# Linear attention and a Strassen MLP in float32 on one core: a longer software pipeline in attention, earlier fetches of weight pieces, later loads of values

## The chip, the core and the metric

The kernel runs on one core of one Trainium2 chip. The metric is the device time of one execution in microseconds (us). It stood at 1071.13 us before the change, the median of three runs (1074.04, 1069.88 and 1071.13). The engines are named as the profile names them: PE is TensorE's matrix multiply and PEld its weight load, DVE is VectorE, ACT is ScalarE, POOL is GpSimd, and SP is the engine whose queue issues nearly all DMAs.

## The reference

Eight batches of eight heads, 576 rows, 64 columns. Attention by 128 random features, then a rank-32 mixing over the rows, then an MLP:

```python
def phi(x):
    proj = np.einsum('bhsd,md->bhsm', x, omega)
    h = proj - np.sum(x * x, axis=-1, keepdims=True) / 2.0
    h = h - np.max(h, axis=-1, keepdims=True)
    return np.exp(h) / np.sqrt(m)
kv = np.einsum('bhsm,bhsd->bhmd', k_p, v)
z = np.sum(k_p, axis=2)
num = np.einsum('bhsm,bhmd->bhsd', q_p, kv)
den = np.einsum('bhsm,bhm->bhs', q_p, z)[..., None] + 1e-06
x = num / den                                  # then [batch, row, head * 64 + column]
u = x + (x.transpose(0, 2, 1) @ U @ V).transpose(0, 2, 1)
out = u + np.maximum(u @ w_ch1, 0.0) @ w_ch2
```

q, k, v and omega are float32. U, V, w_ch1 (512 x 2048) and w_ch2 (2048 x 512) are float64 and are brought to float32 on the chip.

## The kernel before, in words

The program has two stages. Up to about 315 us of the profile it is attention, with the mixing of finished batches and the first part of the weight decoding woven in. From about 345 us to the end it is the MLP, as seven-product (Strassen) block multiplications. The change touches attention alone.

**Units, rounds and steps.** A unit is a pair of batches and a pair of heads; there are 16. Its 2 x 576 rows make nine tiles of 128 rows, one of which (tile 4) holds rows of both batches. Round r works on one unit's keys and one unit's queries side by side, tile by tile, so that there are 16 x 9 = 144 steps (`Step`, lines 728 to 770). Round 0 has two units' keys, the last round two units' queries. One step goes through this chain:

- `turn`, `high`, `low` (lines 610 to 622), once for three tiles: DVE transposes the raw rows into `xT`, ACT rounds them to `xh`, POOL makes the remainder `xl`.
- `project` (lines 734 to 743): six PE matmuls into one PSUM bank `p_p` (two banks, taken in turn), three for keys and three for queries.
- `peak` (line 749): DVE takes the negated maxima `nm` from the bank.
- `exp` (line 756): four ACT activations from the bank into the SBUF tile `e` (a ring of two), the queries' half first.
- `use`: for keys (line 653) two PE matmuls add `e` times the values `vt` (or `vm` in tile 4) to `p_kv`; for queries (line 679) PE transposes `e` into `p_q`.
- `copy` (line 684): DVE or ACT, by the step's parity, copies `p_q` into the SBUF tile `eT` (a ring of four).
- `combine` (lines 692 and 699): PE multiplies `eT` by the finished key sums `kv` into `p_n`.
- `finish` (lines 709 to 726): DVE takes reciprocals (`rec`) and normalizes into `x`.

**What sets the order.** The loop over s (line 826) runs through the steps with a table `DELAY`: at position s the operation `op` is written for step s - DELAY[op]. The order in which a position's operations are written is fixed: turns, copies, exponentials of the queries, norms, exponentials of the keys, mixing, use of the queries, project, use of the keys, peak, combine. A scheduler then makes each engine's instruction list: it takes the written order as priority but lets an instruction that it reckons ready pass one that it reckons waiting. Each engine works its list in order and stops at the first instruction that has to wait.

**Loads.** All loads of a round stand in SP's list. At positions t = 0 and 1 of round r come 16 DMAs of the next keys (`kt`) and queries (`qt`) (line 594). At t = 4 and 5 come the next keys' values (`load_values`, lines 632 to 643, six DMAs `vt` and `vm`). The tiles of values are two, and a third at the start in a spare tile `x`, so a load has to wait until the keys two units earlier are through with their tile.

**Weight decoding.** `decoding` (line 125) is a generator that is advanced once in some steps (two of three at first, later one of two). A piece of float64 words is fetched by SP into one of two tiles `raw` (line 195; 512 KB for a piece of w1), ACT makes its magnitude and its low word (`magnitude`, lines 132 and 135), and DVE follows in three instructions, one for each advance (lines 150, 151, 154). The third is the last reader of `raw`. For the first 11 pieces (`wide`) two empty advances follow, and at the fifth the next fetch into the tile is written:

```python
if j == len(slots) - 1:
    fetch(i + 1 + depth())
```

**Mixing.** When a pair of batches is through, `mixing` (line 390) adds the rank-32 product in 512-column matmuls (lines 446, 411 and 414), DVE adds x into the tile `ut` (line 422, a ring of two), and SP stores it to DRAM.

Of the kernel before, what the change touches and what calls it, by code (L numbers as in the profile page):

```python
# [29 lines left out]
def performer_mlp_kernel(ctx: ExitStack, tc, q, k, v, omega, U, V, w1, w2, out):  # L30
# [85 lines left out]
    def decoding(jobs, late, lean, base, hold=(), defer=(), wide=0):  # L116
# [25 lines left out]
        for i, job in enumerate(jobs):  # L142
# [21 lines left out]
            for j, slot in enumerate(slots):  # L164
# [6 lines left out]
                if j == len(slots) - 1:  # L171
                    fetch(i + 1 + depth())
# [217 lines left out]
    def mixing(pair, x, last):  # L390
# [272 lines left out]
    class Queries(Part):  # L663
# [18 lines left out]
        def copy(self, s):  # L682
            self.eT[s] = wk.tile([P, 2, P], F32, name="eT", bufs=4)
            (nc.vector.tensor_copy if (s + self.place) % 2 else nc.scalar.copy)(out=self.eT[s], in_=self.pq.pop(s))  # L684
# [43 lines left out]
    class Step:  # L728
# [17 lines left out]
        def peak(self):  # L746
# [5 lines left out]
            self.e = wk.tile([P, 4, P], F32, name="e", bufs=2)  # L752
# [56 lines left out]
    for j in range(2):  # L809
# [8 lines left out]
        "turn0": 0, "copy": 5, "turn1": 0, "exp1": 4, "norm": 7, "exp0": 4,  # L818
        "kvfin": 5, "high0": 0, "low0": 1, "high1": 1, "low1": 1, "use1": 4,
        "project": 2, "use0": 4, "peak": 3, "combine": 6,  # L820
    }
    steps = {}
# [3 lines left out]
    for s in range(NR * NT + 7):  # L826
# [3 lines left out]
        if r + 1 < NR:  # L830
# [11 lines left out]
            if t in (4, 5) and not last:  # L842
                new[0].load_values(t - 4)
# [11 lines left out]
        at = lambda op: steps.get(s - DELAY[op])  # L855
        for p in at("turn0").group(0) if at("turn0") else []:
            p.turn()
        if s % (3 if s < 6 * NT else 2):
            advance(decoder)
        st = at("copy")  # L860
        for p in st.queries() if st else []:
            p.copy(st.s)
        for p in at("turn1").group(1) if at("turn1") else []:
            p.turn()
        if at("exp1") and at("exp1").n > 1:
            at("exp1").exp(1)
        st = at("norm")
        for p in st.queries() if st else []:
            if st.s == 0 and p.hp == 0:
                x = xp.tile([P, NT, DM], F32, name="x")  # L870
            p.finish(st.s, x)
            if st.s == 1 - p.last and p.hp == NU - 1:
                mixers.append(mixing(p.pair, x, p.last))
        if at("exp0"):
            at("exp0").exp(0)
        st = at("kvfin")
        for p in st.parts if st and st.s == NT - 1 else []:
            if isinstance(p, Keys):
                p.finish()
        for p in at("high0").group(0) if at("high0") else []:  # L880
            p.high()
        for p in at("low0").group(0) if at("low0") else []:
            p.low()
# [519 lines left out]
```

## Time and profile before

| what | value |
|---|---|
| time, three runs | 1074.04, 1069.88, 1071.13 us; median 1071.13 |
| the profiled execution's own time | 1071.45 us |
| span of the profiled execution, first to last instruction | 1069.5 us |
| outside the span | 1071.45 - 1069.5 = 1.95 us |
| PE busy over the span | 1036.0 us (97%) |
| DVE, ACT, POOL busy | 867.7 us (81%), 614.5 us (57%), 504.1 us (47%) |
| mean granted PE clock | 0.992 |

How to read it: matmuls overlap in the array, so PE's busy time is the union of durations that each hold a pipeline's latency; a PE that is 97% busy can still be short of matmuls. PEld, the time in which weights are being loaded, falls sooner when the list stalls. A wait is shown in brackets at the row of the instruction that waited, with what ended it. The granted clock is 1.00 or 0.50 at any one time; a stage's value is its mean.

### The profile page before, as it was taken

The numbers are of one execution on the slowest core, as the hardware profiler recorded it, in microseconds if no ns is written. First come the engines' busy times: TensorE is split into PE (matmuls) and PEld (weight loads), VectorE is DVE, ScalarE is ACT, GpSimd is POOL, SyncE is SP. The second block draws the span as 40 slices with busy tenths as digits, with TensorE's granted clock in tenths as the row PEclk, the third lists the DMA queues.
The fourth block names the chain that finished last, engine by engine and source line by source line (L and its number), as shares of the span: only waits on it lengthen the run. The fifth ranks groups of instructions, "written<-read, shape, count | busy, mean of one in ns | idle before, by whom it ended". The sixth has DMA issues, their size and how long they took to land. (4 is left out here: it accounts for less than half of the span.)

```text
span 1069.5 us, 23886 instructions
## 1 busy us (share of the span) xinstructions
PE 1036.0 (97%) x8497; PEld 1013.1 (95%) x8497; DVE 867.7 (81%) x1510; ACT 614.5 (57%) x1479; POOL 504.1 (47%) x453
## 2 busy tenths in 40 slices
PE   8899999999998889999999999999999999999998
PEld 7888899989987789999999999999999999999998
DVE  4787898897898976676677476779999999999995
ACT  5887889988874546445355354655344444444442
POOL 3445866866433623233233324535745545545543
PEclk9998999999999999999999999999999999999999
DMA  9688578585335765887677856964455355454451
GB/s 132 137 148 162 107 179 165 119 196 111 85 90 133 194 178 128 225 226 180 192 203 180 226 160 205 313 212 160 167 177 168 131 176 169 138 172 165 139 172 46
DMA packets 380486, 175.51 MB, mean 164 GB/s; under 512 B 275664, under 2 KB 353488, under 8 KB 375760
## 3 DMA queue, kind: packets, MB, share of 16 engines
q1 hardware_dynamic: 378000, 173.70, 61.9%
q8 instruction: 67, 1.10, 0.4%
q10 hardware_dynamic: 2368, 0.30, 0.2%
q14 instruction: 51, 0.42, 0.1%
HBM read 109.97 MB, written 63.96 MB: 163 GB/s over the span
## 5 line engine op out<-in xcount | busy, mean ns | idle before, releaser
L756 ACT ACTIVATE e<-p_p,nm 128x128 f32<-128x128 f32 x576 | 166.9, 396 | 29.6 <-DVE nm L749 22.9
L1176 ACT CAST gh<-gs 128x512 fp32r<-128x512 f32 x140 | 86.7, 621 | 153.7 <-DVE gs L1150 83.1
L1150 POOL TENSOR_TENSOR gs<-graw 128x512 f32<-128x512 f32 x70 | 104.8, 1504 | 145.1 <-DMA graw<-g 88.5
L943 ACT ACTIVATE g<-g 128x512 f32<-128x512 f32 x105 | 66.4, 632 | 165.2 <-DVE g L947 106.3
L622 POOL TENSOR_TENSOR xl<-xT,xh 128x384 fp32r<-128x384 f32 x96 | 97.0, 1027 | 113.0 <-ACT xh L618 101.6
L1183 DVE TENSOR_TENSOR gl<-gs,gh 128x512 fp32r<-128x512 f32 x140 | 134.8, 971 | 15.4 <-ACT gh L1176 13.6
L749 DVE TENSOR_REDUCE nm<-p_p 128x4 f32<-128x512 f32 x144 | 98.1, 681 | 28.7 <-PE p_p L743 17.7
L174 POOL TENSOR_TENSOR wf<-wf,low 128x512 int32<-128x512 int32 (+2 forms) x35 | 45.1, 1289 | 141.3 <-ACT g L943 120.6
L741 PE MATMUL p_p<-omh,xh 128*128 128x256 f32 x288 | 93.8, 326 | 3.2 <-ACT e L756 1.7
L1262 POOL TENSOR_TENSOR u<-u,p 128x256 f32<-128x256 f32 x72 | 74.8, 1068 | 33.3 <-DVE u L1262 30.7
L1176 ACT CAST gh<-graw 128x512 fp32r<-128x512 f32 x107 | 63.9, 619 | 36.9 <-PE p_q L1337 8.9
L1183 DVE TENSOR_TENSOR gl<-graw,gh 128x512 fp32r<-128x512 f32 x107 | 81.1, 773 | 4.9 <-ACT gh L1176 4.0
L743 PE MATMUL p_p<-omh,xl 128*128 128x256 f32 x288 | 82.7, 288 | 0.6 <-POOL xl L622 0.6
L742 PE MATMUL p_p<-oml,xh 128*128 128x256 f32 x288 | 82.3, 286 | 0.0
L1337 PE MATMUL p_p<-wh,gh 128*128 128x256 f32 x288 | 81.1, 282 | 0.0
L1337 PE MATMUL p_p<-wh,gl 128*128 128x256 f32 x288 | 81.0, 281 | 0.0
L1337 PE MATMUL p_p<-wl,gh 128*128 128x256 f32 x288 | 80.9, 281 | 0.0
L699 PE MATMUL p_n<-kv,eT 128*128 128x65 f32 x512 | 73.2, 273 | 6.8 <-ACT eT L684 2.9
L699 PEld LDWEIGHTS p_n<-kv,eT 128*128 128x128 f32 x512 | 68.1, 195 | 10.6 <-ACT eT L684 3.3
L1337 PE MATMUL p_q<-wh,gh 128*128 128x256 f32 x276 | 77.7, 282 | 0.0
L1337 PE MATMUL p_q<-wh,gl 128*128 128x256 f32 x276 | 77.7, 281 | 0.0
L1337 PE MATMUL p_q<-wl,gh 128*128 128x256 f32 x276 | 77.5, 281 | 0.0
(267 smaller groups left out, 4019.3 us busy)
## 6 DMA issues: line engine op xcount, KB each, us to landing
graw<-g SPq DMA_DIRECT2D x36, 1024.0 KB, 5.3
g<-g SPq DMA_DIRECT2D x282, 128.0 KB, 2.4
raw<-in_moe_w_ch_dram SPq DMA_DIRECT2D x22, 512.0 KB, 4.8
u_dram<-ut SPq DMA_DIRECT2D x36, 256.0 KB, 2.4
u<-u_dram SPq DMA_DIRECT2D x36, 256.0 KB, 2.7
out_dram<-u SPq DMA_DIRECT2D x36, 256.0 KB, 2.4
kt<-in_k_dram SPq DMA_DIRECT2D x120, 72.0 KB, 2.7
qt<-in_q_dram SPq DMA_DIRECT2D x120, 72.0 KB, 2.6
```

Of the source, the lines that this page charges most:

```text
L622: nc.gpsimd.tensor_tensor(out=self.xl[-1], in0=self.turned, in1=f32(self.xh[-1]), op=ALU.subtract)
L699: nc.tensor.matmul(pn[:, h, :], eT[:, h, :], kv[:, h, s // 5, :], start=True, stop=True)
L741: nc.tensor.matmul(o, part.xh[g][:, ts], oh, start=True, stop=False)
L742: nc.tensor.matmul(o, part.xh[g][:, ts], ol, start=False, stop=False)
L743: nc.tensor.matmul(o, part.xl[g][:, ts], oh, start=False, stop=True)
L749: nc.vector.tensor_reduce(out=self.nm[:, :n], in_=self.pp[:, :n], axis=AX.X, op=ALU.max, negate=True)
L756: nc.scalar.activation(out=self.e[:, j, :], in_=self.pp[:, j, :], func=AF.Exp, bias=self.nm[:, j : j + 1])
L1150: K(engine.tensor_tensor(out=to, in0=self.val[x], in1=self.val[y], op=op))
L1176: K(nc.scalar.copy(out=h, in_=v))
L1183: K(nc.vector.tensor_tensor(out=l, in0=v, in1=f32(h), op=ALU.subtract))
L1262: K(engine.tensor_tensor(out=out, in0=x, in1=y, op=ALU.add))
L1337: K(nc.tensor.matmul(acc[bank][:, half, :], x[:, ks], y[:, f, :], start=(now.s == 0 and k == 0 and half == 0 and x is h and y is wh), stop ...
```

## The change

Six edits, all in attention:

1. `DELAY` grows: use 4 to 5, copy 5 to 6, `kvfin` (ACT's copy of the finished key sums) 5 to 6, combine 6 to 8, norm 7 to 9. Turns, project (2), peak (3) and exp (4) stay.
2. Over the last 18 steps the delays fall by one for every three steps until they are what they were (`SHORT`), so that the loop still ends at the same position. A position can hold an operation of two steps there.
3. The rings grow with it: `e` from two to three, `eT` from four to six. `p_p` stays at two banks, `p_q` at two.
4. `load_values` moves from t = 4 and 5 to t = 7 and 8 (`VT` is the delay of the keys' use plus two; it was that delay itself).
5. The fetch of a raw piece, for the first 11 pieces, is written behind the third advance of the piece that leaves the tile, and not behind its fifth.
6. The ring of `ut` grows from two to three.

```diff
-                if j == len(slots) - 1:
+                if j == (2 if i < wide else len(slots) - 1):
                     fetch(i + 1 + depth())
...
-                ut = mp.tile([P, DM], F32, name="ut", tag=tag, bufs=2)
+                ut = mp.tile([P, DM], F32, name="ut", tag=tag, bufs=3 if tag == "ut" else 2)
...
-            self.eT[s] = wk.tile([P, 2, P], F32, name="eT", bufs=4)
+            self.eT[s] = wk.tile([P, 2, P], F32, name="eT", bufs=6)
...
-            self.e = wk.tile([P, 4, P], F32, name="e", bufs=2)
+            self.e = wk.tile([P, 4, P], F32, name="e", bufs=3)
...
-        "project": 2, "use0": 4, "peak": 3, "combine": 6,
+        "project": 2, "use0": 5, "peak": 3, "combine": 8,
     }
+    SHORT = {"copy": 5, "norm": 7, "kvfin": 5, "use1": 4, "use0": 4, "combine": 6}
+    CLOSE = NR * NT - 18
+
+    def delay(op, k):
+        return max(SHORT.get(op, DELAY[op]), DELAY[op] - max(0, (k - CLOSE + 3) // 3))
+
+    VT = DELAY["use0"] + 2
...
-            if t in (4, 5) and not last:
-                new[0].load_values(t - 4)
+            if t in (VT, VT + 1) and not last:
+                new[0].load_values(t - VT)
...
-        at = lambda op: steps.get(s - DELAY[op])
...
+        def at(op):
+            for k in range(s - DELAY[op], s - SHORT.get(op, DELAY[op]) + 1):
+                if k in steps and k + delay(op, k) == s:
+                    yield steps[k]
```

The rest of the diff turns each `if at(op)` of the loop into `for st in at(op)`.

What the scheduler makes of it is seen in the engines' lists. First SP's list in the third and fourth round, before the change. `kt` and `qt` are the 16 loads of a round, `vt` and `vm` its values, `raw` a piece of w1:

```order
L594 DMA kt<-in_k_dram 32x18x32 x8
L594 DMA qt<-in_q_dram 32x18x32 x8
L636 DMA vt_120<-in_v_dram 128x4x64 x2
L640 DMA vm_121<-in_v_dram 64x2x64
L636 DMA vt_120<-in_v_dram 128x4x64 x2
L640 DMA vm_121<-in_v_dram 64x2x64
L195 DMA raw<-in_moe_w_ch_dram 128x1024
L594 DMA kt<-in_k_dram 32x18x32 x8
L594 DMA qt<-in_q_dram 32x18x32 x8
L636 DMA vt_122<-in_v_dram 128x4x64 x2
L640 DMA vm_123<-in_v_dram 64x2x64
L195 DMA raw<-in_moe_w_ch_dram 128x1024
```

The same place of SP's list after the change:

```order
L594 DMA kt<-in_k_dram 32x18x32 x8
L594 DMA qt<-in_q_dram 32x18x32 x8
L195 DMA raw<-in_moe_w_ch_dram 128x1024
L636 DMA vt_120<-in_v_dram 128x4x64 x2
L640 DMA vm_121<-in_v_dram 64x2x64
L636 DMA vt_120<-in_v_dram 128x4x64 x2
L640 DMA vm_121<-in_v_dram 64x2x64
L594 DMA kt<-in_k_dram 32x18x32 x8
L594 DMA qt<-in_q_dram 32x18x32 x8
L195 DMA raw<-in_moe_w_ch_dram 128x1024
L636 DMA vt_122<-in_v_dram 128x4x64 x2
```

The first piece of w1 has passed six loads of values and the second has passed three; the loads of keys and queries stand where they stood.

Then PE's list around step 104, before. Here `e_4050` and `eT_4114` belong to step 104, `e_4089` to step 105, and `p_p_4078` to the projection of step 106:

```order
L743 MATMUL p_p_4078<-omh_115,xl_4000 128x256
L653 MATMUL p_kv_3912<-vt0_120,e_4050 128x65 [waits DMAHW3_49]
L653 MATMUL p_kv_3912<-vt0_120,e_4050 128x65 [waits DMAHW4_49]
L699 MATMUL p_n_4174<-kv_3544,eT_4114 128x65 [waits DVE_49,Activation_49]
L699 MATMUL p_n_4174<-kv_3544,eT_4114 128x65
L679 MATMUL p_q_4130<-ident_100,e_4089 128x128 [waits Activation_49] x2
L741 MATMUL p_p_4133<-omh_115,xh_3970 128x256 [waits Activation_49]
```

And after, where `e_4034` and `eT_4132` are step 104's, `e_4073` step 105's, `e_4128` step 106's, and `p_p_4117` is the projection of step 107:

```order
L679 MATMUL p_q_4138<-ident_100,e_4073 128x128 [waits PE_49,Activation_49]
L679 MATMUL p_q_4138<-ident_100,e_4073 128x128 [waits Activation_49]
L741 MATMUL p_p_4117<-omh_115,xh_3947 128x256 [waits DVE_49,Activation_49]
L742 MATMUL p_p_4117<-oml_116,xh_3947 128x256
L743 MATMUL p_p_4117<-omh_115,xl_3977 128x256
L741 MATMUL p_p_4117<-omh_115,xh_3979 128x256
L742 MATMUL p_p_4117<-oml_116,xh_3979 128x256
L743 MATMUL p_p_4117<-omh_115,xl_3981 128x256
L653 MATMUL p_kv_3916<-vt0_120,e_4034 128x65 [waits DMAHW3_49]
L653 MATMUL p_kv_3916<-vt0_120,e_4034 128x65 [waits DMAHW4_49]
L699 MATMUL p_n_4221<-kv_3554,eT_4132 128x65 [waits DVE_49,PE_49]
L699 MATMUL p_n_4221<-kv_3554,eT_4132 128x65
```

The use of step 104's keys and its combine have moved behind the projection of step 107; the transposes of step 105 stand, as before, between the projections of steps 106 and 107. Counted over steps 10 to 125 (116 steps), the newest projection ahead of a step's transposes is the next step's in all 116 cases in both lists. Ahead of the use of a step's keys it is that of two steps on in all 116 cases before, and of three (114) or four (2) after. Ahead of a combine it is that of two steps on 86 times and of three 30 times before, 76 times and 40 times after. ACT's and DVE's copies stand by the same exponentials and maxima as before, bar single cases. Behind attention PE's list is the same, row by row, apart from buffer numbers.

More of the change, by code (lines that the diff above doesn't have):

```diff
@@ L854, in performer_mlp_kernel @@
             early.todo.append(None)
[L855 to L857 removed]
+        def at(op):
+            for k in range(s - DELAY[op], s - SHORT.get(op, DELAY[op]) + 1):
+                if k in steps and k + delay(op, k) == s:
+                    yield steps[k]
+        for st in at("turn0"):
+            for p in st.group(0):
+                p.turn()
         if s % (3 if s < 6 * NT else 2):
@@ L859, in performer_mlp_kernel @@
             advance(decoder)
[L860 to L883, printed above, removed]
-        for p in at("high1").group(1) if at("high1") else []:
-            p.high()
+        for st in at("copy"):
+            for p in st.queries():
+                p.copy(st.s)
@@ new lines, in performer_mlp_kernel @@
+        for st in at("turn1"):
+            for p in st.group(1):
+                p.turn()
+        for st in at("exp1"):
+            if st.n > 1:
+                st.exp(1)
+        for st in at("norm"):
+            for p in st.queries():
+                if st.s == 0 and p.hp == 0:
+                    x = xp.tile([P, NT, DM], F32, name="x")
+                p.finish(st.s, x)
+                if st.s == 1 - p.last and p.hp == NU - 1:
+                    mixers.append(mixing(p.pair, x, p.last))
@@ L886, in performer_mlp_kernel @@
+        for st in at("exp0"):
+            st.exp(0)
+        for st in at("kvfin"):
+            for p in st.parts if st.s == NT - 1 else []:
+                if isinstance(p, Keys):
+                    p.finish()
+        for st in at("high0"):
+            for p in st.group(0):
+                p.high()
+        for st in at("low0"):
+            for p in st.group(0):
+                p.low()
+        for st in at("high1"):
+            for p in st.group(1):
+                p.high()
         if mixers:
@@ L888, in performer_mlp_kernel @@
                 mixers.pop(0)
-        for p in at("low1").group(1) if at("low1") else []:
-            p.low()
-        if at("use1") and at("use1").n > 1:
-            at("use1").use(1)
-        if at("project"):
-            at("project").project()
-        if at("use0"):
-            at("use0").use(0)
-        if at("peak"):
-            at("peak").peak()
-        st = at("combine")
-        for p in st.queries() if st else []:
-            p.combine(st.s)
+        for st in at("low1"):
+            for p in st.group(1):
+                p.low()
+        for st in at("use1"):
+            if st.n > 1:
+                st.use(1)
+        for st in at("project"):
+            st.project()
+        for st in at("use0"):
+            st.use(0)
+        for st in at("peak"):
+            st.peak()
+        for st in at("combine"):
+            for p in st.queries():
+                p.combine(st.s)
         if mixers:
```

4 lines of the change are left out of this document (2 added, 2 removed).

## The prediction

> **What bounds the kernel now.** The page comes first, for the size of things.
>
> ```profile
> PE 1036.0 (97%) x8497; PEld 1013.1 (95%) x8497; DVE 867.7 (81%) x1510; ACT 614.5 (57%) x1479; POOL 504.1 (47%) x453
> ```
>
> PE bounds the whole, but the change touches attention alone, so the stages have to be read apart. The table of engines by stage (busy us and instructions in brackets for PE, PEld, DVE, ACT and POOL, then the granted clock, the DMA share and GB/s):
>
> ```profile
> core 0 of [0], span 1069.5 us
> ...
> 12.00:45.00 33.00, 30.42 (x235) 28.61 (x234) 19.52 (x43) 26.11 (x87) 11.80 (x12) 0.95 0.71 132
> 45.00:95.00 50.00, 44.14 (x350) 42.41 (x351) 41.24 (x102) 38.20 (x129) 19.57 (x20) 0.93 0.81 153
> 95.00:235.00 140.00, 136.90 (x1115) 128.93 (x1114) 127.44 (x304) 126.15 (x405) 105.52 (x110) 1.00 0.73 153
> 235.00:313.00 78.00, 75.96 (x633) 73.90 (x633) 67.17 (x172) 67.19 (x217) 39.12 (x38) 0.98 0.49 104
> 345.00:1069.50 724.50, 711.32 (x5964) 708.74 (x5962) 580.80 (x823) 338.72 (x605) 311.44 (x246) 1.00 0.60 178
> ```
>
> The last row, 724.5 us, is the MLP; PE's list is unchanged there and I count it as it is. In the four attention rows (301 us) the weight load is the engine nearest to full, with 301 - (28.61 + 42.41 + 128.93 + 73.90) = 27.2 us idle. That is the pool from which a better order can take. DVE and ACT are at 85 to 91% in the third row, so no one engine is a hard wall there: PE, DVE and ACT wait for each other around the chain project, maxima, exponentials. The groups of weight loads say where PE's list stops (window 12 to 315 us; behind the last bar the idle time before the group and what ended it):
>
> ```profile
> L653 PEld LDWEIGHTS p_kv<-vt,e 128*128 128x128 f32 x480 | 64.8, 195 | 0.7 <-ACT kv L659 0.4 <-ACT e L756 0.3
> L699 PEld LDWEIGHTS p_n<-kv,eT 128*128 128x128 f32 x480 | 64.2, 195 | 8.8 <-ACT eT L684 3.3 <-ACT e L756 2.1 <-DVE eT L684 0.9
> ...
> L741 PEld LDWEIGHTS p_p<-omh,xh 128*128 128x128 f32 x284 | 55.0, 194 | 7.9 <-ACT e L756 5.9 <-ACT xh L618 1.2
> ...
> L679 PEld LDWEIGHTS p_q<-ident,e 128*128 128x128 f32 x276 | 38.7, 167 | 6.6 <-ACT e L756 4.2
> ```
>
> So 8.8 us stand at combine, 7.9 at projection, 6.6 at the queries' transposes and 0.7 at the keys' use. Of the four, the lists move only combine and the keys' use, and the keys' use has nothing to give.
>
> The single large waits come from the timelines. ACT:
>
> ```profile
> 68.06 0.67 ACT L132 ACTIVATE wf<-raw 128x512 f32<-128x512 f32 x1 [0.87 <-DMA raw<-in_moe_w_ch_dram]
> ...
> 81.79 0.66 ACT L132 ACTIVATE wf<-raw 128x512 f32<-128x512 f32 x1 [1.19 <-DMA raw<-in_moe_w_ch_dram]
> 82.36 0.64 ACT L135 ACTIVATE low<-raw 128x512 int32<-128x512 uint32 x1
> 82.90 0.35 ACT L684 COPY eT<-p_q 128x256 f32<-128x256 f32 x1
> ```
>
> And PE behind them:
>
> ```profile
> 70.16 0.59 PE L679 MATMUL p_q<-ident,e 128*128 128x128 f32 x2 [1.08 <-ACT e L756]
> ...
> 83.31 0.66 PE L699 MATMUL p_n<-kv,eT 128*128 128x65 f32 x4 [2.10 <-ACT eT L684]
> ```
>
> ACT stands still until a raw piece lands, then runs its two decoding activations, and only then the copy or the exponentials for which PE waits. The second of these costs more than its 2.10 us, as the table of short stretches shows (same columns):
>
> ```profile
> 67.20:70.60 3.40, 2.32 (x19) 2.01 (x18) 2.59 (x9) 2.54 (x8) 1.70 (x2) 1.00 1.11 141
> 80.90:84.30 3.40, 1.19 (x9) 0.84 (x8) 1.46 (x6) 2.51 (x8) 1.33 (x2) 1.00 0.96 163
> 84.30:91.10 6.80, 6.75 (x33) 6.75 (x34) 3.94 (x9) 4.32 (x15) 1.97 (x2) 0.50 0.76 120
> 237.90:241.30 3.40, 1.36 (x13) 1.34 (x13) 2.85 (x10) 3.40 (x12) 3.40 (x5) 1.00 0.90 144
> 241.30:244.70 3.40, 3.40 (x20) 3.40 (x19) 1.78 (x5) 2.26 (x8) 0.94 (x2) 0.50 0.92 226
> ```
>
> Behind a stretch in which PE was busy for 1.19 us of 3.40 the granted clock is 0.50 for 6.8 us, in which PE is busy throughout and ACT only for 4.32. The same follows at 241.3 us. Behind the stretch from 67.2 us, with 2.32 us busy, the clock stayed at 1.00. The Trainium skill ("TensorE: Matmul & The Clock Gate", section "Why this matters for your kernels") asks for PE gaps over about 3 us before the clock falls back; the trace disagrees, since 2.10 us was enough. By that rule the slow stretch would have some other cause and term 3 below would be nought.
>
> **The change part by part.** SP's rows around the two late pieces:
>
> ```profile
> 59.62 1.05 SPq L636 DMA_DIRECT2D vt<-in_v_dram  x2
> ...
> 63.27 0.53 SPq L195 DMA_DIRECT2D raw<-in_moe_w_ch_dram  x1
> ...
> 74.96 0.99 SPq L636 DMA_DIRECT2D vt<-in_v_dram  x2
> ...
> 76.75 0.82 SPq L195 DMA_DIRECT2D raw<-in_moe_w_ch_dram  x1
> ```
>
> *Term 1, first piece.* In the new list it stands where the values stood, at 59.62 and not 63.27, which is 3.65 us earlier. It landed when ACT began at 68.06, so it would land near 64.4. ACT's 0.87 us wait goes. Of the 1.08 us that PE then waited I take 0.87. Bounds 0 and 1.08.
>
> *Term 2, second piece.* 74.96 in place of 76.75, 1.79 us earlier; it landed at 81.79, so near 80.0, against an ACT that is free at 81.79 - 1.19 = 80.60, or 79.7 if term 1 is handed on. The wait of 1.19 us goes, with 0.2 us left of it at most, say 1.1 us off PE's 2.10. Bounds 0 and 2.10.
>
> *The fetch's own wait.* At its new place a fetch waits on SP for DVE's third instruction on the piece that leaves the tile, and the values, or some of the next loads, are queued behind it. DVE's rows for the two tiles:
>
> ```profile
> 46.50 0.46 DVE L154 SCALAR_TENSOR_TENSOR wf<-raw,wf 128x288 uint32<-128x288 uint32 x1
> ...
> 61.17 1.27 DVE L154 SCALAR_TENSOR_TENSOR wf<-raw,wf 128x288 uint32<-128x288 uint32 x1
> ```
>
> The tiles are free at 46.96 and 62.44, over 12 us ahead of 59.62 and 74.96, so nothing is held. That cover gone, SP would wait for DVE by up to one advance, about 3 us at two advances in three steps, and the values with it.
>
> *Term 3, the clock.* With term 2 PE would be busy about 1.19 + 1.1 = 2.3 us in the stretch from 80.90, like the one at 67.2 that kept the clock. At full clock the 6.75 us of half-clock PE work need 3.4 us, DVE 3.94 and ACT 4.32, so ACT would bind: 6.80 - 4.32 = 2.5 us. The window's phase can spoil it; I take 2.0. Bounds 0 and 3.4.
>
> *Term 4, combine.* The 8.8 us at L699 contain the 2.10 us of term 2 and this one:
>
> ```profile
> 239.99 0.63 PE L699 MATMUL p_n<-kv,eT 128*128 128x65 f32 x4 [2.04 <-ACT e L756]
> ```
>
> And on ACT, ahead of it:
>
> ```profile
> 238.95 0.39 ACT L684 COPY eT<-p_q 128x256 f32<-128x256 f32 x1
> 239.21 1.18 ACT L756 ACTIVATE e<-p_p,nm 128x128 f32<-128x128 f32 x4
> ```
>
> In the new list the transposes of step 105 and the projection of step 107 come ahead of this combine. But they read, or wait for, the exponentials of step 105, and on ACT those stand behind the copy (239.21 after 238.95). PE would stop at the transposes instead and go on at about the same moment. I give this wait 0.2 us, and leave the half clock behind it. The rest of L699, 8.8 - 2.10 - 2.04 = 4.7 us, is many small waits. Combine moves behind one more projection in a net 10 of 116 steps, some 9%; where it does, its wait is gone, and elsewhere the later combine also keeps PE's list from stopping ahead of the next projection. I take 0.8 us. Bounds of both together: -1 (the 10 shift other waits forward) and 4.7 + 2.04 = 6.7.
>
> *Nothing expected.* The keys' use a step later: 0.7 us idle in all, covered then by a step of distance and now by two. Projection and transposes: their place relative to the exponentials is the same in 116 of 116 steps, so the 7.9 and 6.6 us stay except for what terms 1 to 3 take. The rings of `e`, `eT` and `ut`: what waits for a free `ut` is not among the waits, and the other two only keep pace with the longer delays. If that cover went, the next late thing would be ACT's exponentials, as now.
>
> *Values.* They are issued later, but their waits at SP shrink. Now:
>
> ```profile
> SPq L636 <- PE p_kv L653: 23.8, 8, 5.9
> ```
>
> Between 100 and 320 us SP is held 23.8 us, in eight waits, at values whose tile the keys still use; stores and the next 16 loads are queued behind. No engine waits for those, so taking it away is worth nothing. The price is early, where SP has no gap. The median landing of the values in the first 100 us (behind the size), an early load and the first use:
>
> ```profile
> vt<-in_v_dram SPq DMA_DIRECT2D x24, 128.0 KB, 2.9
> ...
> 46.30 1.09 SPq L636 DMA_DIRECT2D vt<-in_v_dram  x2
> ...
> 53.03 0.66 PE L653 MATMUL p_kv<-vt,e 128*128 128x65 f32 x4 [0.26 <-ACT kv L659]
> ```
>
> Values issued at 46.30 land by 46.30 + 1.09 + 2.9 = 50.3 us, and the round's first use is at 53.03. The new list puts U's and V's or a w1 piece ahead of them, 0.5 to 1.9 us; the use is also one step later. Cost 0; bounds 0 and 1.5.
>
> *Filling and closing.* The pipeline is a step longer from projection to use, and closes up at the end. The first steps are bound by loads anyway. Since the last 18 steps hold the same work, I put 0.3 us; bounds -0.5 and one step, which is 301 us of the four stages over 144 steps, 2.1 us.
>
> *Sum.* 0.9 + 1.1 + 2.0 + 0.2 + 0.8 - 0.3 = 4.7 us. The profiled execution took 1071.45 us (span 1069.5 and 1.95 around it), which is 0.3 us over the median of 1071.13. So 1071.45 - 4.7 = 1066.75, less 0.3 gives 1066.4; I say 1066. Without the clock term it would be 1068.4.
>
> **The rivals.** *No change.* The waits for exponentials (5.9 us at projection, 4.2 at the transposes) hang on the two banks of `p_p` and on ACT's order, which the change leaves alone; what terms 1 and 2 save is waited for again at the next exponentials. For it: the counts of the lists, which hardly move. Against it: a landed piece is worth ACT's own time, and ACT is the engine waited for. Time 1069 to 1071.5. The Trainium skill ("Perfetto Trace Analysis", "Optimization Strategy") reads repeated bubbles as too few PSUM or SBUF buffers for the next tile; here that buffer would be `p_p`, and deeper rings elsewhere would not help.
>
> *Much faster.* Every large wait is a chance meeting of decoding on ACT with a combine or a copy. With more distance fewer meet, and a third of the 27.2 us goes, 9 us, with term 3's 2.0: 1071.13 - 11 = 1060. For it: the many small waits, 17 at the projection alone (sum, count, longest):
>
> ```profile
> PEld p_p L741 <- ACT e L756: 5.9, 17, 0.6
> ```
>
> Against it: the 116 of 116.
>
> *Slower.* The values come too late. They now stand right ahead of the next round's 16 loads, in the stretch where SP works without a gap. If SP slips by more than the 2.7 us between 50.3 and 53.03, PE stops at the keys' use at the head of a round, and everything queued on PE behind it, the next projection first. That is 1 to 2 us in each of the four rounds between 45 and 95 us, and behind two of them the half clock at 2.5 us each: 4 x 1.5 + 5 = 11, less the 4 us of terms 1 to 3, or 1078. For it: the DMA share of 0.81. Against it: the use is a step (2.1 us) later too.
>
> **How the numbers follow.** The forecast (1062.5 to 1068.5) gets 0.48, no change 0.21, much faster 0.22, slower 0.09. About 0.5%, 5.4 us, is what a measurement of this kernel can tell from no change, so faster means under 1065.8 and slower over 1076.5. Half of the forecast's chance lies under 1065.8: faster 0.24 + 0.22 = 0.46. Slower is 0.11, the rival with a little for mishaps elsewhere. The rest, 0.43, is the same. The range has to take in no change (1071.5, and 1 us for the runs' spread) and most of much faster: 1058.5 to 1072.5, which leaves out the slower rival and the far end of the fast one. The forecast's own range is 1062.5 to 1068.5.
>
> **What would show it.** Terms 1 and 2 are right if no ACT row at L132 waits for a w1 piece between 60 and 85 us, and the combine behind it waits under 1.2 us; term 3, if the clock is 1.00 from 80 to 91 us. Term 4 is right if L699's idle falls from 8.8 us to between 4 and 7 while L741 and L679 keep 10 to 14 together; if those two fall below 8, the much faster rival holds. Waits of L653 for a DMA at the head of a round would show the slower one. I would be wrong about the stage if the stretch behind 345 us changed by over 2 us.

## The result and the profile after

| kernel | executions | median us | lowest to highest |
|---|---|---|---|
| before | 5 | 1071.13 | 1069.80 to 1074.04 |
| after | 5 | 1064.61 | 1062.63 to 1066.09 |

The ratio is 0.9939, 95% interval 0.9922 to 0.9956, or 6.5 us less; 1066.0 was forecast, in a range of 1058.5 to 1072.5. The profiled execution of the change took 1066.09 us, with a span of 1064.2 us. In a second comparison, beside some of the experiments below, the same change gave 0.9976 (0.9955 to 0.9997). So the 6.5 us are the larger of two measurements, and a part of this text is about why they differ. One execution of before (2608.26 us) and one of the change not closing up (1083.03 us) were in a slower state; ratios, intervals and means leave them out.

The table of engines by stage, as shown of before (busy us for PE, PEld, DVE, ACT and POOL, granted clock, DMA share, GB/s):

```profile
core 0 of [0], span 1064.2 us
...
12.00:45.00 33.00, 30.51 (x213) 29.09 (x213) 19.54 (x42) 25.19 (x85) 11.60 (x12) 0.84 0.71 132
45.00:95.00 50.00, 48.51 (x420) 46.74 (x419) 44.93 (x114) 43.88 (x147) 23.55 (x25) 1.00 0.83 152
95.00:235.00 140.00, 136.65 (x1106) 128.38 (x1105) 128.18 (x308) 126.92 (x408) 108.50 (x113) 1.00 0.78 159
235.00:313.00 78.00, 76.73 (x641) 73.69 (x641) 68.17 (x175) 64.76 (x210) 37.10 (x35) 1.00 0.47 101
345.00:1064.20 719.20, 709.80 (x5922) 707.37 (x5921) 570.54 (x810) 335.44 (x600) 304.64 (x241) 0.99 0.60 177
```

The second row has changed most: 420 matmuls in place of 350 in the same 50 us, and a clock of 1.00 in place of 0.93. The first row is worse than before (0.84), since in this execution the clock was 0.50 from 15.4 to 25.6 us; rounds 0 and 1 together still take 36.7 us, against 36.8 before. The last row is no longer at 1.00.

A profile of this program is read best by its rounds. The start of the maxima (L749) of every ninth step gives the length of each round, here in us for the two profiles:

| round | 0 | 1 | 2 | 3 | 4 | 5 | 6 | 7 to 9 | 10 | 11 | 12 to 14 | 15 (8 steps) |
|---|---|---|---|---|---|---|---|---|---|---|---|---|
| before | 16.6 | 20.2 | 17.7 | 22.7 | 18.8 | 22.7 | 18.6 | 55.9 | 19.0 | 20.7 | 54.7 | 17.7 |
| after | 19.2 | 17.5 | 17.8 | 17.7 | 18.5 | 21.1 | 17.8 | 56.4 | 19.1 | 19.5 | 55.4 | 16.3 |

The largest gain is in round 3, 5.0 us. The last maxima start at 308.7 us and not at 317.3, and the MLP's first matmul at 323.8 and not 332.6: 8.8 us. At the end of the span 5.3 us of these are left. The weight loads by group (window 12 to 315 us, idle time behind the last bar):

```profile
L699 PEld LDWEIGHTS p_n<-kv,eT 128*128 128x128 f32 x503 | 66.1, 192 | 4.9 <-DVE eT L684 1.4 <-ACT eT L684 1.3 <-DVE x L724 0.8
L653 PEld LDWEIGHTS p_kv<-vt,e 128*128 128x128 f32 x480 | 65.5, 198 | 0.0
...
L741 PEld LDWEIGHTS p_p<-omh,xh 128*128 128x128 f32 x284 | 54.7, 193 | 7.8 <-ACT e L756 6.9
...
L679 PEld LDWEIGHTS p_q<-ident,e 128*128 128x128 f32 x288 | 39.6, 161 | 5.9 <-ACT e L756 2.1 <-DVE eT L684 0.3
```

The idle time at combine (L699) has fallen from 8.8 to 4.9 us; projection (L741) and transposes (L679) keep 13.7 of 14.5. SP's two fetches and ACT's reads of the pieces:

```profile
59.27 0.43 SPq L195 DMA_DIRECT2D raw<-in_moe_w_ch_dram  x1
...
74.84 0.43 SPq L195 DMA_DIRECT2D raw<-in_moe_w_ch_dram  x1
```

```profile
67.28 0.68 ACT L132 ACTIVATE wf<-raw 128x512 f32<-128x512 f32 x1
...
79.40 0.68 ACT L132 ACTIVATE wf<-raw 128x512 f32<-128x512 f32 x1
```

Neither row shows a wait any more. The stretches that stood at half clock before:

```profile
80.90:84.30 3.40, 3.19 (x27) 2.98 (x28) 2.15 (x6) 2.51 (x10) 0.00 (x0) 1.00 1.14 155
84.30:91.10 6.80, 6.80 (x64) 6.80 (x63) 6.77 (x19) 6.14 (x22) 1.97 (x2) 1.00 0.79 133
```

PE works without a gap, at 64 matmuls in 6.8 us in place of 33. What is given back lies behind attention. PE's two long stops in the MLP's opening, and what stands ahead of the first on SP, ACT and DVE:

```profile
335.07 0.41 SPq L195 DMA_DIRECT2D raw<-in_moe_w_ch_dram  x1
...
341.25 0.67 ACT L132 ACTIVATE wf<-raw 128x512 f32<-128x512 f32 x1 [1.52 <-DMA raw<-in_moe_w_ch_dram]
...
341.96 0.68 DVE L150 TENSOR_SCALAR wf<-wf 128x512 f32<-128x512 f32 x1 [1.02 <-ACT wf L132]
...
343.29 0.58 PE L979 MATMUL p_n<-uh,wh 128*128 128x256 f32 x1 [2.48 <-DVE g L967]
...
360.96 0.58 PE L979 MATMUL p_kv<-wh,wh 128*128 128x256 f32 x1 [2.77 <-DVE g L967]
```

The same places before the change:

```profile
343.85 0.41 SPq L195 DMA_DIRECT2D raw<-in_moe_w_ch_dram  x1
...
348.47 0.68 ACT L132 ACTIVATE wf<-raw 128x512 f32<-128x512 f32 x1
...
350.71 0.39 PE L959 MATMUL p_n<-uh,wh 128*128 128x256 f32 x1 [1.11 <-DVE g L947]
...
368.29 0.39 PE L959 MATMUL p_kv<-wh,wh 128*128 128x256 f32 x1 [1.13 <-DVE g L947]
```

The raw piece was issued 11.3 us behind the MLP's first matmul in both. Before, ACT read it 4.62 us later without a wait; after, ACT waited for it to land and read it 6.18 us behind its issue. ACT waits, DVE's clamp waits for ACT, the addition that frees PE's bank is queued behind the clamp, and PE stops for 2.48 us in place of 1.11.

### The profile page after: what moved, and what is told of

Read it like the earlier page. It is cut to its first block, busy times and chain, and to the rows that moved or that the text cites. A ratio compares the mean times of both kernels' runs of the same rounds, so it can differ in the third digit from the quotient of the medians.

```text
span 1064.2 us, 23868 instructions
## 1 busy us (share of the span) xinstructions
PE 1038.4 (98%) x8497; PEld 1015.6 (95%) x8497; DVE 862.9 (81%) x1510; ACT 613.5 (58%) x1479; POOL 503.9 (47%) x453
## 5 line engine op out<-in xcount | busy, mean ns | idle before, releaser
L749 DVE TENSOR_REDUCE nm<-p_p 128x4 f32<-128x512 f32 x144 | 98.1, 683 | 28.5 <-PE p_p L743 13.8
L741 PE MATMUL p_p<-omh,xh 128*128 128x256 f32 x288 | 93.7, 325 | 3.5 <-ACT e L756 3.4
L1282 POOL TENSOR_TENSOR u<-u,p 128x256 f32<-128x256 f32 x72 | 74.8, 1067 | 34.0 <-DVE u L1282 31.4
L1203 DVE TENSOR_TENSOR gl<-graw,gh 128x512 fp32r<-128x512 f32 x107 | 80.9, 772 | 7.2 <-ACT gh L1196 6.3
L1357 PE MATMUL p_p<-wl,gh 128*128 128x256 f32 x288 | 80.9, 281 | 0.0
L979 PE MATMUL p_n<-uh,wh 128*128 128x256 f32 x256 | 73.2, 286 | 2.7 <-DVE g L967 2.5
L699 PE MATMUL p_n<-kv,eT 128*128 128x65 f32 x512 | 72.2, 270 | 2.8 <-DVE rec L710 1.1
```

Of the source, the lines that this page charges most:

```text
L741: nc.tensor.matmul(o, part.xh[g][:, ts], oh, start=True, stop=False)
L749: nc.vector.tensor_reduce(out=self.nm[:, :n], in_=self.pp[:, :n], axis=AX.X, op=ALU.max, negate=True)
L979: K(nc.tensor.matmul(p[:, f, :], x[:, k, fs], y[:, k, :], start=first, stop=(k == 1 and y is ul), skip_group_check=True,))
L1203: K(nc.vector.tensor_tensor(out=l, in0=v, in1=f32(h), op=ALU.subtract))
L1282: K(engine.tensor_tensor(out=out, in0=x, in1=y, op=ALU.add))
L1357: K(nc.tensor.matmul(acc[bank][:, half, :], x[:, ks], y[:, f, :], start=(now.s == 0 and k == 0 and half == 0 and x is h and y is wh), stop ...
```

## The experiments

All twelve are listed here with their measurements; the sections below take them in groups. Half clock is the time for which an execution ran at 0.50, worked out from its span and mean clock: span x 2 x (1 - clock), as a mean over the executions. The last column is the mean time less 0.31 us for each us of half clock, which takes out what goes with the clock; where the 0.31 comes from is told in the second group. Where an edit itself makes PE stop more often, this column takes out a part of the edit's own cost too. On the four chips before stands at 1064.5 to 1065.2 in it.

| kernel | median us | ratio to before, 95% | half clock us | mean at equal clock |
|---|---|---|---|---|
| before (115 executions beside the others) | 1070.05 to 1071.74 | 1 | 18.9 | 1064.8 |
| the change (17 executions) | 1064.61; 1069.20 | 0.9939 (0.9922 to 0.9956); 0.9976 (0.9955 to 0.9997) | 18.6 | 1061.8 |
| early fetch alone | 1068.36 | 0.9983 (0.9965 to 1.0000) | 15.3 | 1063.8 |
| late values alone | 1068.83 | 0.9994 (0.9975 to 1.0013) | 14.6 | 1064.2 |
| distance alone | 1077.45 | 1.0065 (1.0043 to 1.0086) | 34.4 | 1066.0 |
| change without early fetch | 1066.77 | 0.9979 (0.9956 to 1.0002) | 19.2 | 1062.0 |
| change, values at t = 5 and 6 | 1067.61 | 0.9977 (0.9952 to 1.0002) | 19.4 | 1062.5 |
| change, not closing up | 1072.25 | 1.0014 (0.9992 to 1.0036) | 25.7 | 1064.1 |
| change, matmuls on zeros | 1066.76 | 0.9973 (0.9948 to 0.9998) | 14.1 | 1063.8 |
| before, one clamp out | 1067.63 | 0.9970 (0.9954 to 0.9986) | 17.2 | 1062.1 |
| change, the clamp out | 1066.14 | 0.9958 (0.9943 to 0.9974) | 16.0 | 1061.1 |
| change, the clamp on POOL | 1069.06 | 0.9987 (0.9967 to 1.0007) | 18.7 | 1063.3 |
| early fetch, the clamp out | 1066.21 | 0.9964 (0.9942 to 0.9985) | 11.9 | 1063.2 |

### The parts of the change

*Early fetch alone*: the kernel before, with

```diff
-                if j == len(slots) - 1:
+                if j == (2 if i < wide else len(slots) - 1):
```

> The kernel before with edit 5 alone (a raw piece is fetched behind the third advance); delays, rings and the place of the values are the old ones. SP's list has the first two w1 pieces ahead of the values, as after the change. Theory A (the raw pieces carry the gain: two ACT waits of 0.87 and 1.19 us, and the half clock behind the second): 1071.1 - 4.3 = about 1067, ACT's rows at L132 between 60 and 85 us without a wait, clock 1.00 from 80 to 91 us, round 3 (maxima of step 27 to 36) at 18 us in place of 22.7. Rival B (the longer distances carry it): over 1069.5, and round 3 near 21 or more. Rival C (every reordering only shakes the small meetings of ACT's work): the gain of this run and that of the longer pipeline alone do not add up to the change's 6.5 us within 2 us.

ACT's two reads, without a wait, and round 3 at 17.9 us, as theory A had it:

```profile
69.15 0.71 ACT L132 ACTIVATE wf<-raw 128x512 f32<-128x512 f32 x1
...
81.18 0.70 ACT L132 ACTIVATE wf<-raw 128x512 f32<-128x512 f32 x1
```

But the time is only 0.17% lower, at the edge of what the runs tell, and not 0.4%: 3 us of the 4.8 that round 3 gains in the profile are not in the executions. In this profile itself a part is lost again: round 10 takes 21.2 us in place of 19.0, and from the first to the last maxima it is 303.0 us against 305.2. The median, 1068.36 us, lies between theory A's 1067 and rival B's 1069.5.

*Late values alone*: the kernel before, with

```diff
-            if t in (4, 5) and not last:
-                new[0].load_values(t - 4)
+            if t in (6, 7) and not last:
+                new[0].load_values(t - 6)
```

> The kernel before with the loads of values two positions later (t = 6 and 7) and nothing else. The first two w1 pieces then stand ahead of the values in SP's list, with edit 5 left out; from the third on a piece stands behind the round's keys and queries. Theory A: the same as the early fetch alone, about 1067 (1066 to 1068), no ACT wait at L132 between 60 and 85 us. Rival B: over 1069.5. If the late values had a price at the head of a round (waits of L653 for a DMA between 45 and 95 us), it would show here at up to 1.5 us, since the use stands at its old place.

Round 3 is 18.5 us, and no read of a w1 piece waits; the time is the same as before within the interval, and again between theory A's 1068 and rival B's 1069.5. So which of the two edits puts the piece ahead of the values doesn't matter, and neither is worth 4 us by itself.

*Distance alone*: the change without these two edits. The longer delays, their closing up and the rings stay.

```diff
-                if j == (2 if i < wide else len(slots) - 1):
+                if j == len(slots) - 1:
...
-            if t in (VT, VT + 1) and not last:
-                new[0].load_values(t - VT)
+            if t in (4, 5) and not last:
+                new[0].load_values(t - 4)
```

> The change without edit 5 and with the values at their old positions t = 4 and 5: the longer delays, their closing up and the rings alone. SP's list has the w1 pieces and values in the old order. Theory A: ACT waits for raw pieces near 68 and 82 us as before, half clock behind the second, round 3 at 21 to 23 us; the distance gives 0.7 to 2.5 us elsewhere, so 1068.5 to 1070.5. Rival B: 1064 to 1067, with round 3 at 18 to 19 us although the pieces come late, because a combine two steps later no longer meets the copy that waits. Rival C: any value, with gains that do not add up with those of the fetch alone.

It is 0.65% slower, which neither theory A nor rival B had; rival C allowed any value. Its profile shows what a late piece does in the longer pipeline (timelines of ACT and PE, then two stretches):

```profile
67.06 0.66 ACT L132 ACTIVATE wf<-raw 128x512 f32<-128x512 f32 x1 [1.18 <-DMA raw<-in_moe_w_ch_dram]
```

```profile
69.15 0.73 PE L679 MATMUL p_q<-ident,e 128*128 128x128 f32 x2 [1.55 <-ACT e L756]
```

```profile
66.00:69.40 3.40, 1.84 (x14) 1.46 (x12) 2.58 (x8) 2.34 (x7) 1.50 (x2) 1.00 1.06 137
69.40:79.60 10.20, 10.16 (x49) 9.86 (x49) 5.47 (x12) 5.25 (x18) 2.69 (x3) 0.50 0.84 167
```

PE stops at the transposes, now ahead of the combine in its list, and runs at half clock for 10.2 us behind a stop of 1.55 us. Round 3 takes 23.2 us. Over the twelve executions half clock is 34.4 us; of the 6.6 us that the mean is above before's in the same runs (1076.68 against 1070.11), 0.31 x (34.4 - 18.1) = 5.1 go with the clock.

*Change without early fetch*:

```diff
-                if j == (2 if i < wide else len(slots) - 1):
+                if j == len(slots) - 1:
```

> The change without edit 5; the values still come at t = 7 and 8, which alone puts the first two w1 pieces ahead of the values. Theory A: edit 5 is not needed, 1064 to 1066, like the change itself. If edit 5 carries something of its own (the third and fourth piece inside the round's loads of keys), 1067 or more, with an ACT wait at L132 behind 85 us. Rival B: like the change, 1064 to 1066.

0.9979, and 0.9976 for the whole change: edit 5 adds nothing to the later values that these runs can tell (each interval is over 4 us wide). Round 3 is 17.9 us.

*Values at t = 5 and 6*: the change with

```diff
-    VT = DELAY["use0"] + 2
+    VT = DELAY["use0"]
```

> The change with the values loaded at t = 5 and 6, at the moment at which the longer delay frees their tile, in place of t = 7 and 8. SP's list still has the w1 pieces ahead of the values, since edit 5 is in. Theory A2: as the change, ratio 0.993 to 0.997, round 3 at 18 us, no ACT wait for a w1 piece between 60 and 85 us; SP is held at the values again (some 24 us in place of 21), which costs nothing. If the two positions carry something of their own: over 0.998.

0.9977: as long as the pieces are ahead of the values, their place costs and brings nothing that these runs can tell.

*Not closing up*: the change with

```diff
-    SHORT = {"copy": 5, "norm": 7, "kvfin": 5, "use1": 4, "use0": 4, "combine": 6}
+    SHORT = {}
...
-    for s in range(NR * NT + 7):
+    for s in range(NR * NT + 9):
...
-        elif t == 7:
+        elif t == 7 and r == NR - 1:
```

> The change without edit 2: the delays stay long to the end and the loop runs two positions further. The last round's maxima do not move (16.3 us for the last eight steps as after the change, if the shorter last round comes from the distance), but the last combine and what hangs on it, the mixing and the MLP's first matmul, come later by 1 to 2 of the steps of 2.1 us, partly under other work: +1 to +4 us against the change. If the closing is worth nothing: within 1 us of the change.

1.0014, or a mean of 1072.1 against the change's 1068.8 on the same chip: closing up is worth 3.3 us (95% interval 1.1 to 5.5), of which 0.31 x (25.7 - 19.9) = 1.8 go with the clock. Its profiled execution took 1083.03 us, the longest of its twelve, so no size is read from that trace.

Taken together, the parts do not add: in their runs the means moved by -1.6 (fetch) and +6.6 us (distance), and the whole by -2.6. That is the sign which rival C named. The distance loses time with late pieces. That it gains with early ones is not shown: with it and without it the ratios are 0.9976 and 0.9983 for the early fetch, 0.9979 and 0.9994 for the late values, and the intervals overlap. Rival B, that the distance carries the gain, falls; theory A holds for the place and fails for the sum.

### The change once more, and the clock

> The changed kernel once more, unaltered, so that it stands beside the others on the same chip with a second profile. Theory A2 (the early raw pieces and the longer distance only pay together: late pieces in the longer pipeline stop PE at the transposes and cost clock): ratio 0.993 to 0.996 to the kernel before, and the half-clock time of its executions (span x 2 x (1 - mean clock)) at 10 to 17 us on average, against 18 in the 35 executions of the kernel before. If it is nearer 0.998, the three parts only differ by chance.

0.9976, with half clock of 19.9 us in the mean: both lie outside what theory A2 gave. The ratio is the one nearer to 0.998, for which the text above had said that the three parts then differ only by chance. Over all executions with a known clock, before has 6.4 to 36.5 us of half clock, 18.9 in the mean, and the time rises by 0.31 us for each us of it (115 executions, correlation 0.71). For the change it is 6.4 to 27.8, 18.6 in the mean, with the same slope of 0.31 (17 executions). So **the change does not lower the half-clock time; at equal clock it is 3.0 us faster** (1064.8 against 1061.8; on this chip alone 2.7, give or take 1.3). The executions of before spread from 1065.0 to 1076.1 us, and half-clock time goes with half of their variance (0.71 squared). That is a correlation: a stop of PE costs time itself and can bring half clock behind it, and these figures do not part the two.

One large place of half clock is in round 5. In this second profile of the change (one timeline, all engines):

```profile
116.71 2.54 POOL L401 TENSOR_TENSOR ml<-x,mh 128x512 fp32r<-128x512 f32 x2
...
118.32 5.05 DVE L150 TENSOR_SCALAR wf<-wf 128x512 f32<-128x512 f32 x1
...
119.19 0.76 POOL L255 TENSOR_TENSOR wl<-wf,wh 128x256 fp32r<-128x256 f32 x1
...
119.89 1.98 POOL L622 TENSOR_TENSOR xl<-xT,xh 128x384 fp32r<-128x384 f32 x2
...
121.81 1.28 POOL L401 TENSOR_TENSOR ml<-x,mh 128x512 fp32r<-128x512 f32 x1
...
125.11 0.48 PE L679 MATMUL p_q<-ident,e 128*128 128x128 f32 x1 [3.07 <-ACT e L756]
```

DVE's clamp of a raw piece takes 5.05 us, from 118.32 to 123.37, while POOL works without a gap until 121.81 + 1.28 = 123.09. The maxima and the exponentials stand behind it, and PE stops for 3.07 us. The stretch behind it, in the table of stretches:

```profile
124.00:130.80 6.80, 5.69 (x27) 5.59 (x28) 4.48 (x11) 4.59 (x16) 1.96 (x2) 0.50 0.29 60
```

In the first profile of the change, and in that of before, the same instruction took

```profile
118.59 1.24 DVE L150 TENSOR_SCALAR wf<-wf 128x512 f32<-128x512 f32 x1
```

```profile
125.85 3.03 DVE L150 TENSOR_SCALAR wf<-wf 128x512 f32<-128x512 f32 x1
```

Over the first ten profiles of the study: 3.03 to 3.06 us in all three with the old delays (round 5 at 22.7 to 22.8 us, clock at 1.00), and with the new ones 5.05 to 5.08 us in four of seven (round 5 at 24.2 to 25.0, half clock behind it) and at most 1.5 in three (round 5 at 21.1). The profile of the change that came with the result is one of these three. That is 3.9 us in round 5 and 1.3 in round 6 which an execution of the change has or has not.

### The meeting of DVE and POOL

Two kernels leave this one clamp out, by

```diff
             if i < wide:
                 slots += [None] * (5 - len(slots))
+            if wide and i == 6:
+                slots[0] = None
```

> The kernel before without one instruction: the clamp of the exponents (DVE L150) of the seventh raw piece, whose values it doesn't change. The engines' lists are otherwise the same, row by row. In the three profiles with the old delays this instruction took 3.03 to 3.06 us beside POOL, in place of 0.4 to 0.5, and PE waited 1.33 to 1.36 us behind it, with no half clock. Theory D (this meeting of DVE and POOL costs what its stop of PE costs): round 5 falls from 22.7 us to about 21, the time by 1.5 us, ratio 0.998 to 0.999. Rival E (the next meeting takes its place): round 5 stays over 22, ratio 0.9995 or more.

> The change without the same one instruction; the engines' lists are otherwise the change's, row by row. With the new delays it took 5.05 to 5.08 us in four of seven profiles (PE then waited 3.1 us, half clock for up to 6.8 us behind it, rounds 5 and 6 together 43 to 44 us), and at most 1.5 us in three (38.9 us). Theory D: rounds 5 and 6 at 38 to 39 us, and the mean of the executions 2 to 3 us under the change's, ratio to the kernel before 0.994 to 0.996, half-clock time 15 to 17 us on average in place of 20. Rival E: rounds 5 and 6 at 42 us or more in this profile too, or the time as the change's (0.9976) since clock and stops come up elsewhere.

Before: round 5 is 21.2 us and the ratio 0.9970. With the change: rounds 5 and 6 are 20.9 and 18.0 us and the ratio is 0.9958. Theory D holds for the place in both, and for the size with the change. For the kernel before it had 0.998 to 0.999, 1.5 us, and the mean fell by 3.0 us; the interval, 0.9954 to 0.9986, holds a part of both, and where the rest would come from is open. So the instruction of 0.4 us costs some 3 us of the kernel before and 2 of the change, the latter across two chips. With it out, the change stands at a mean of 1066.07 against 1067.43. These 1.4 us, give or take 1.4, are what the change is worth beside this meeting, and about as much as twelve executions of each can tell.

*The clamp on POOL*, which leaves nothing out:

```diff
-                lambda: nc.vector.tensor_scalar(m, m, _LEAST, _MOST, ALU.max, ALU.min),
+                lambda: (nc.gpsimd if wide and i == 6 else nc.vector).tensor_scalar(m, m, _LEAST, _MOST, ALU.max, ALU.min),
```

> The change with that clamp of the seventh piece as an instruction of POOL, which computes the same. POOL then runs it in its own row, and DVE has nothing there that can be held for 5 us; the lists of PE, ACT and DVE move in some places over the next rounds. Theory D: as without the clamp, plus up to 0.5 us if DVE waits for POOL's result: ratio 0.994 to 0.997. Rival E: 0.9976 or more. If DVE's next instruction on the piece (L151) waits for POOL more than 2 us, PE stops as before and nothing is won.

0.9987, nothing won. Round 5 is 24.4 us, and rounds 5 and 6 together take 41.2 in place of 38.9 in the first profile of the change, since the piece's next DVE instruction now meets POOL's row (0.64 us at this place in the first profile of the change):

```profile
125.11 2.76 DVE L151 TENSOR_SCALAR wf<-wf 128x512 uint32<-128x512 uint32 x1
```

PE's longest stop there is 0.88 us, without half clock, so PE does not stop as it did. Rival E holds for this cure, and not for the meeting's price.

*Early fetch, the clamp out*: the edit of early fetch alone and the two lines that leave the clamp out, both on the kernel before.

> The kernel before with edit 5 alone and without the clamp of the seventh raw piece (which doesn't change its values): the early raw pieces with the old distances, freed of the meeting of DVE and POOL. So far, against the kernel before: without the clamp 0.997, the whole change without the clamp 0.9958, edit 5 alone 0.9983. Theory F (the distance brings 5 us by the end of attention, as 295 in place of 300 us from the first to the last maxima, and loses most of it again behind, so that net it is worth under 1 us): 0.9955 to 0.9965, that is 0.997 less the 0.001 to 0.0015 of the early pieces; last maxima near 312 us, and the stretch from there to the end 753 to 754 us. Theory A3 (what distance gains stays): 0.9965 to 0.998, clearly over the whole change's 0.9958.

0.9964, inside what theory F named; but the interval, 0.9942 to 0.9985, holds the other theory as well. The last maxima start at 310.9 us, and 307.0 in the change without the clamp, yet the medians are 1066.21 and 1066.14. What the distance adds in the end is small by this and not settled.

### The half clock in the MLP's opening

```diff
+    spots = {(0, 1, 3, 0): (7, "p_q"), (0, 1, 5, 0): (7, "p_q"), (1, 0, 5, 0): (7, "p_p")}
+
+    def filler(*spot):
+        n, tag = spots.get(spot, (0, None))
+        if n:
+            room = ps.tile([P, P], F32, name="warm_" + tag, tag=tag, bufs=2)
+        for _ in range(n):
+            K(nc.tensor.matmul(room, idle, idle, start=True, stop=True))
...
+                filler(c, g, i, f)
```

> The change plus 21 matmuls on a tile of zeros, seven each (about 1.5 us) ahead of the three products of the MLP's opening at which PE stops for DVE's additions: product 11 (343.29, 2.48 us in the profile after), product 13, and product 20 (360.96, 2.77 us). If it is the half clock behind these stops (343 to 346 and 360 to 367 us) that gives back part of the gain: the windows between 340 and 370 us go, and the time falls by 1 to 3 us against the change. If the clock falls all the same, or PE was not the bound in those windows: 0 to +1.5 us, the matmuls' own time where no stop covers it.

The two stretches at half clock, in the change and then with the matmuls on zeros:

```profile
339.60:343.00 3.40, 1.22 (x11) 1.01 (x9) 2.38 (x6) 1.35 (x3) 1.92 (x2) 1.00 0.74 210
343.00:346.50 3.50, 3.21 (x15) 3.21 (x16) 3.47 (x5) 1.10 (x2) 2.34 (x3) 0.51 0.79 252
360.10:366.90 6.80, 5.94 (x28) 5.95 (x29) 5.41 (x10) 4.49 (x11) 3.33 (x5) 0.50 0.75 165
```

```profile
339.60:343.00 3.40, 3.11 (x26) 2.92 (x26) 2.35 (x6) 1.71 (x3) 1.59 (x2) 1.00 0.65 191
343.00:346.50 3.50, 2.87 (x24) 2.87 (x25) 3.47 (x5) 1.10 (x2) 2.36 (x2) 1.00 0.84 262
360.10:366.90 6.80, 5.59 (x50) 5.40 (x49) 5.41 (x10) 4.48 (x11) 3.10 (x4) 1.00 0.93 211
```

The clock stays at 1.00, and the first 28 products take 54.2 us, against 53.8 in the change. DVE is as busy as in the change to 0.01 us in the last two stretches, which fits DVE setting the pace there; PE's clock costs nothing that the trace shows. The means, 1068.2 against 1068.8 us for the change on the same chip, can't tell the two apart. Another trace says the same: the change without early fetch has no half clock between 327.4 us and the MLP's last matmul, and its MLP takes 736.8 us, no less than the 736.6 in the change. The half clock is not what the MLP gives back.

## Why the prediction came out right, step by step

**Terms 1 and 2 were right.** The pieces were fetched at 59.27 and 74.84 us (59.62 and 74.96 forecast), and neither read's row shows a wait. Round 3 is 17.5 to 18.5 us in ten profiles that have the pieces ahead of the values (an eleventh is the one not read for sizes), and 22.7 to 23.2 in the three that have them behind (before, before without the clamp, distance alone).

**Term 3 was right for the place and wrong as a term of the sum.** In the profile the clock is 1.00 from 80.9 to 91.1 us, and round 3 gains 5.0 us, where terms 1 to 3 had 4.0. But the step took the half clock of one profiled execution as a fixed cost. The mean half clock of an execution is 18.9 us before and 18.6 after, so the 2.0 us of this term are not there in the mean. The sum without it, 4.7 - 2.0 = 2.7 us, is close to the 3.0 us measured at equal clock, and to the 2.6 us of the second comparison; how far that is luck is told below. That the first comparison gave 6.5 us is partly a matter of these executions: their half clock was 15.3 us in the mean, against 19.9 in the second comparison, which at 0.31 is worth 1.4 us. The rest of the difference is open.

**Term 4 was right in its bounds and wrong in one step.** L699's idle is 4.9 us (4 to 7 forecast) and L741 and L679 keep 13.7 (10 to 14). The step "PE would stop at the transposes instead and go on at about the same moment" failed: it does stop there, but for a third of the time,

```profile
232.84 0.59 PE L679 MATMUL p_q<-ident,e 128*128 128x128 f32 x2 [0.69 <-ACT e L756]
```

and not for 2.04 us. The half clock that was to be left at 241 us has gone, and round 11 is 1.2 us shorter.

**Values: right.** No use of the keys waits for a DMA between 45 and 95 us, and moving the loads back changes nothing that the runs can tell (0.9977 against 0.9976). The slower rival has no trace.

**Filling and closing: the size was off.** The forecast cost 0.3 us; the last round is 1.4 us shorter, and without closing up 3.3 us are lost, 1.8 of them with the clock.

**The stage behind attention: wrong.** "PE's list is unchanged there and I count it as it is", with 2 us as the bound. From the first to the last matmul the MLP takes 733.1 us before and 736.6 after, 3.5 more. It took 733.1 to 735.4 us in the five profiles with the old delays (mean 734.3), and 734.2 to 738.4 in the six with the new ones that close up, have the pieces early and no matmuls on zeros (mean 736.2). Between before and after no engine's list differs there. The late landing is not enough to explain it. Of the 3.5 us, 1.5 come in the first 28 products, which take 52.3 us before and 53.8 after, and 2.0 come behind them. And in the other four profiles with the old delays these products take 53.9 to 54.1 us, as they do after the change: it was before's own profile that ran quickly here. What makes the MLP longer with the new delays stays open.

**Luck in the total.** The forecast of 1066 us lies between the two measurements, 1064.61 and 1069.20, but not for the sum's reasons alone. In the profiles that came with the result the MLP began 8.8 us earlier, where the sum had 4.7 us, and the MLP gave 3.5 us back, where the sum had nothing. Two misses of opposite sign make the total better than its parts.

**Nothing of the forecast had round 5.** The sum has no term for DVE's instruction beside POOL, although the row of 3.03 us stood in the trace of before.

**The rivals.** No change (0.21, ratios of 0.998 to 1) is out by the first interval; by the second, 0.9955 to 0.9997, it is not. The much faster one would have needed L741 and L679 under 8 us; they kept 13.7, and distance alone was slower. One reading slipped without harm to the sum: in the third row of the table of before, DVE and ACT are at 91 and 90%, not at 85 to 91%.

## What to carry to other kernels

Price a stall that a profile shows once by how often it comes up: with the clock known for many executions, the time at equal clock told the change apart from the spread of the executions, and a single trace did not. Look for the instruction that takes several times its usual length (5.05 us in place of 0.4) before looking for another distance; a longer pipeline moves such a meeting and may widen it. Parts depend on each other: the distance cost 0.65% with late pieces and nothing that could be measured with early ones, so undo one part as well as doing one part alone.

## What the runs showed of the hardware

- **DVE beside POOL.** The clamp of a 128x512 piece (L150) takes 0.4 to 0.5 us where it isn't held (16 of its 32 places before), and took 1.24, 3.03 and 5.05 us at this one beside POOL. In the two profiles of the change it ended 0.28 us behind the end of a POOL instruction: 119.83 against 119.55, and 123.37 against 123.09 at the end of POOL's whole row (POOL's times are rough). It is the same elsewhere: in the fourteen traces of this case L150 and L151 took over 0.9 us on a 128x512 piece 330 times, each time with a POOL instruction running when they began, and each time they ended 0.28 to 0.29 us behind the end of a POOL instruction. The Trainium skill ("SBUF — State Buffer", "Who interferes with whom") says that DVE and GpSimd share a pair of ports, that a DVE instruction in a mode with two ports (tensor_scalar, as L150 is, can be in one) contends with GpSimd for it, and that whoever issues first "gets the shared pair for the whole instruction" while the other blocks. The traces agree, and show more than that: one blocked DVE instruction can be passed by four POOL instructions in a row that start after it.
- **Half clock.** Stops of 1.55 us (distance alone, 1.84 us busy in the 3.4 us around it) and of 2.48 us (1.22 us busy) were followed by 0.50; 3.11 us busy in the same stretch kept 1.00. PE's busy time alone does not settle it: with 2.31 us busy in 3.42 (distance alone, from 318.56 us) 0.50 followed, and with 1.63 in 3.42 (second profile of the change, from 376.60 us) 1.00 stayed. One us of half clock went with 0.31 us of time, and with none in the MLP's opening.
- **Landing.** The same 512 KB piece at the same place was waited for and read 6.18 us behind its issue in one profile, and read 4.62 us behind it without a wait in another. What made the difference is open.
